# Where two-tile blocks keep the parts of their tokens in an SBUF buffer

## The chip, the cores and the metric

The kernel runs on one core of one Trainium2 chip. The metric is the device time of one execution in microseconds; for repeated executions the median is given. A profile is one execution with the hardware profiler on; its span runs from the first to the last instruction on the core.

## The reference

The computation is one block of a network on 2048 tokens of width 448, in float32:

- a conditioning vector gives six rows of 448 values (two shifts, two scales and two gates) by a matrix product;
- the tokens are normalised over their width, scaled and shifted, and convolved along the sequence with a kernel that comes from a state-space model; gated, this is added to the tokens;
- the sum is normalised, scaled and shifted again, and goes through a gated feed-forward layer: `(silu(h @ w_gate) * (h @ w_up)) @ w_down`, with 448 x 1792 gate and up weights and 1792 x 448 down weights; gated, this is added again.

The feed-forward layer is the large part, and it is the part that the change is in.

## The kernel before

The 2048 tokens are 16 tiles of 128. They go through the feed-forward layer in six blocks: the first two have two tiles (256 tokens), the last four have three (384 tokens). The hidden width of 1792 is 14 slices of 128, numbered f.

Precision comes from splitting. A value is kept as a high part, in TensorE's one-pass 32-bit format, and a low part, the rest. A product of two values is made of three products: high x high, high x low, low x high. The tokens of a block, transposed so that channels lie on partitions, stand in two SBUF tiles: `hhi` (high parts) and `hlo` (low parts), each of shape 128 x 4 x 384, where the second index k is the group of channels. A weight slice `gu` holds seven 128 x 128 matrices for the gate and seven for the up weights.

For each slice f the function `gate_up` computes the gate and the up product, s = 0 and 1. For each s there are seven matmuls with `hhi` and four with `hlo`, all recorded at line 754. The weights are loaded into the array as the stationary operand (128 columns), and the tokens stream past as the moving operand: 256 columns in a two-tile block, 384 in a three-tile block. So one slice takes 2 x 11 = 22 matmuls. After it, `down` (line 804) adds the slice f - 1 to the outputs: for each tile of the block three matmuls, with the hidden values (`phi`, `plo`) as the stationary operand and 448 columns of down weights (`wdh`, `wdl`) as the moving one. Between slices, single steps for the next block are put in after the slice's matmuls by a table of times: the convolution (lines 976 to 989) and, ahead of the last `down` of a block, the transposes of the next block's tokens (line 227 in one form). The order on TensorE is thus the order of the program. The other engines split weights (lines 115 to 125), apply the activation and split the hidden values (lines 769 to 792).

At the end of the last block `finish` (line 832) does the last two slices of the down product in pieces of 448, 256 and 192 columns, so that results leave earlier. They too have `phi` or `plo` as the stationary operand and down weights as the moving one.

Where a tile lies in SBUF is counted in bytes from the start of a partition. In this program `hhi` and `hlo` begin at bytes 48736 and 54880, both 96 modulo 256; every `gu` tile begins at 32 modulo 256, and so do all `wdh` and `wdl` tiles; `phi` and `plo` begin at 224 modulo 256. The matrices in `gu` (512 bytes each), the groups k in `hhi` (1536 bytes), and the tiles in `phi` (512 bytes) are all multiples of 256 bytes apart, so that a pair of tiles has one distance modulo 256. Counted from the moving to the stationary operand, it is

- (32 - 96) mod 256 = 192 for gate/up in a three-tile block;
- (32 - 224) mod 256 = 64 for gate/up in a two-tile block, since there the tokens begin at column 32 of the buffer, that is at byte 96 + 128 = 224;
- (224 - 32) mod 256 = 192 for the down products, in every block and in `finish`.

Where the parts are written: `high`, `high_v` and `low` for the first block's tokens, `split_turned` for the second block's, `transposes` for all others (lines 219 and 220 inside).

Of the kernel before, what the change touches and what calls it, by code (L numbers as in the profile page):

```python
# [51 lines left out]
def f32(ap):  # L52
    return ap.bitcast(F32)
# [3 lines left out]
def tile_kernel(ctx, tc, x, a_re, a_im, b_re, b_im, c_re, c_im, log_dt,  # L57
                wd, wgate_up, states, groups, vecs, dft, idft, out):
    nc = tc.nc
    sy, ve, sc, po, pe = nc.sync, nc.vector, nc.scalar, nc.gpsimd, nc.tensor  # L60
# [10 lines left out]
    def bank():  # L71
        t = psg.tile([128, 512], F32, name="bank")
        return t
# [38 lines left out]
    def split_d(j, part=None):  # L112
        hi, lo = wp[j]
        if not part:
            sc.copy(hi, wdn[j])
        if part != 0:
            ve.tensor_tensor(lo, wdn[j], f32(hi), op=OP.subtract)

    def split_w(j, part):
        w = raw[j]  # L120
        if part == 0:
            sc.copy(wgu[j][:, :, 0:3, :], w[:, :, 0:3, :])  # L122
            sc.activation(wgu[j][:, :, 3, :], w[:, :, 3, :], AF.Copy, scale=half)  # L123
        else:
            ve.tensor_tensor(wgu[j][:, :, 3:7, :], w[:, :, ::-1, :], f32(wgu[j][:, :, 0:4, :][:, :, ::-1, :]), op=OP.subtract)  # L125
# [18 lines left out]

    sbc = const.tile([128, 4], F32)
    flag = const.tile([1, 1], I32)
    first_col = lambda n: 32 if n == 256 else 0
    hhi = const.tile([128, 4, MB * 128], F32R)
    hlo = const.tile([128, 4, MB * 128], F32R)
    gd = const.tile([128, D], F32)  # L150
# [67 lines left out]
    def parts(hi, lo, src, k):  # L218
        sc.activation(hi, src, AF.Identity, bias=sbc[:, k:k + 1])
        ve.scalar_tensor_tensor(lo, src, sbc[:, k:k + 1], f32(hi), op0=OP.add, op1=OP.subtract)  # L220

    def transposes(ts):
        n = len(ts) * 128
        for k in (0, 2, 1, 3):
            ps = CV if k == 2 else bank()
            for j, i in enumerate(ts):
                pe.transpose(ps[:, j * 128:(j + 1) * 128], xn[i][:, k * 128:(k + 1) * 128], ident)  # L227
            c_ = slice(first_col(n), first_col(n) + n)
            parts(hhi[:, k, c_], hlo[:, k, c_], ps[:, 0:n], k)

    xd = [dram.tile([128, 512], F32, name=f"xd{q}") for q in range(MB)]
# [10 lines left out]
    def split_turned(ts):  # L242
        n, m = len(ts) * 128, len(ts)
        for k in range(4):
            hi, lo = (h[:, k, first_col(n):first_col(n) + n].rearrange("p (q a r) -> p q a r", q=m, a=4) for h in (hhi, hlo))
            parts(hi, lo, turned[:, 0:m, :, k, :], k)

    wp0 = ctx.enter_context(tc.tile_pool(name="wp0", bufs=1))
# [38 lines left out]
    with tc.tile_pool(name="pre", bufs=1) as pre:  # L287
# [153 lines left out]

        def high(q, ks=range(4)):
            for k in ks:
                c_ = slice(32 + q * 128, 160 + q * 128)
                sc.activation(hhi[:, k, c_], pk[q, k][:, k * 128:(k + 1) * 128], AF.Identity, bias=sbc[:, k:k + 1])

        def high_v(q, ks):
            for k in ks:
                c_ = slice(32 + q * 128, 160 + q * 128)
                ve.tensor_scalar(hhi[:, k, c_], pk[q, k][:, k * 128:(k + 1) * 128], sbc[:, k:k + 1], None, op0=OP.add)  # L450

        def low(q, ks=range(4)):
            for k in ks:
                c_ = slice(32 + q * 128, 160 + q * 128)
                ve.scalar_tensor_tensor(hlo[:, k, c_], pk[q, k][:, k * 128:(k + 1) * 128], sbc[:, k:k + 1], f32(hhi[:, k, c_]),
                                        op0=OP.add, op1=OP.subtract)

# [9 lines left out]
        def flag_of():  # L467
# [49 lines left out]
            "fr1": copy(run1[end], CV[end, 0:D]), "fx": copy(xs[0], DN[0][:, 0:D]),  # L517
            "tr0": do(to_channels, 0), "tr1": do(to_channels, 1, (0, 1)), "tr1b": do(to_channels, 1, (2, 3)),
            "hi00": do(high, 0, (0, 1)), "hi01": do(high_v, 0, (2, 3)),
            **{f"hi1{z}": do(high, 1, (2 * z, 2 * z + 1)) for z in range(2)},  # L520
            **{f"lo{q}{z}": do(low, q, (2 * z, 2 * z + 1)) for q in range(2) for z in range(2)},

            "w0": do(split_w, 0, 0), "w01": do(split_w, 0, 1), "w1": do(split_w, 1, 0), "w11": do(split_w, 1, 1),
# [206 lines left out]
    def run_blocks(pools, stages, first=None):  # L730
        work, hid = pools.work, pools.hid
        def ffn(ts, fresh, last, todo):
            n = len(ts) * 128
# [3 lines left out]
            def gate_up(f, nw):  # L737
                head = fresh and f < 2
                if fresh and f:
                    split_d(f)  # L740
                w = wgu[f]
                p = hid.tile([128, 280], F32, name="p") if fresh else p_of[f % 2]
                hi = hid.tile([128, MB * 128], F32R, name="phi")
                lo = hid.tile([128, MB * 128], F32R, name="plo")
                ps = [bank(), bank()]

                top = [(k, a) for k, ws in enumerate(((0, 6), (1, 5), (2, 4), (3,))) for a in ws]
                low = [(k, k) for k in range(4)]  # L750

                def mm(s, ka, lo, first=False, end=False):
                    for q, (k, a) in enumerate(ka):
                        pe.matmul(ps[s][:, 0:n], w[:, s, a], (hlo if lo else hhi)[:, k, first_col(n):first_col(n) + n],  # L754
                                  start=first and q == 0, stop=end and q == len(ka) - 1)

                if head:
                    for k in range(3):
                        for s in range(2):
                            mm(s, [(k, k)], False, k == 0)  # L760
                    for s in range(2):
                        mm(s, [(k, 6 - k) for k in range(3)] + [(3, 3)], False)
                    for s in range(2):
                        mm(s, low, True, False, True)
                else:
                    for s in range(2):
                        mm(s, top, False, True)
                        mm(s, low, True, False, True)
                sc.activation(p[:, 0:n], ps[0][:, 0:n], AF.Silu)  # L769
                for g, a in todo.get((f, 2), []):  # L770
                    g(*a)
                pp[f] = hi, lo
                if last and f == NF - 1:
                    c_ = [slice(q * 128, (q + 1) * 128) for q in range(len(ts))]
                    for q in range(len(ts) + 1):
                        for o in c_[q:q + 1]:
                            ve.tensor_tensor(ps[1][:, o], p[:, o], ps[1][:, o], op=OP.mult)
                            sc.copy(hi[:, o], ps[1][:, o])
                        for o in c_[max(q - 1, 0):q]:
                            ve.tensor_tensor(lo[:, o], ps[1][:, o], f32(hi[:, o]), op=OP.subtract)  # L780
                    return
                if nw is not None:
                    split_w(nw, 0)
                ve.tensor_tensor(ps[1][:, 0:n], p[:, 0:n], ps[1][:, 0:n], op=OP.mult)  # L784
                if fresh and f == 0:
                    split_d(0, 1)
                    for g, a in todo.get("mid", []):
                        g(*a)
                elif nw is not None:
                    split_w(nw, 1)  # L790
                sc.copy(hi[:, 0:n], ps[1][:, 0:n])  # L791
                ve.tensor_tensor(lo[:, 0:n], ps[1][:, 0:n], f32(hi[:, 0:n]), op=OP.subtract)  # L792
                if fresh and f == 0:
                    split_w(nw, 1)
# [11 lines left out]
            m = len(ts) - 1  # L806
# [64 lines left out]
        if first is not None:  # L871
            for i in TILES[1]:
                load_x(i)
            for i in TILES[0]:
                first(i)
                n2.stat(i, TILES[0])
            n2.root(TILES[0])
            for q, i in enumerate(TILES[0]):
                make_xn(i, work.tile([128, 512], F32, name=f"xn{q}"))
            transposes(TILES[0])  # L880
        for b, ts in enumerate(TILES):
            todo = {}
            if b + 1 < len(TILES):
# [40 lines left out]
                if late:  # L924
                    go(late[0], n2.root, nx)
                    for q, (h, i) in enumerate(zip(late[1], nx)):
                        if b:
                            go(h, make_xn, i, xn_of[q])
                        else:
                            go(h, make_xn, i, xn_of[q], 0)  # L930
                            at(NF - 2, 2, make_xn, i, xn_of[q], 1)
                at(NF - 1, 0, transposes if late else split_turned, nx)
            ffn(ts, b == 0, b + 1 == len(TILES), todo)

# [151 lines left out]
def build(nc, aps, out):  # L1086
    with tile.TileContext(nc) as tc:
        a = dict(aps)
        tile_kernel(tc, a["A_u"].rearrange("b l d -> (b l) d"), *[a[n] for n in _INS[1:] + ["B_w_gate_up", "A_states", "w_mod_groups", "c_log_dt", "dft", "idft"]],
                    out.rearrange("b l d -> (b l) d"))  # L1090
# [20 lines left out]
```

## Time and profile before

| | |
|---|---|
| median of 3 runs | 471.81 us (471.29 to 472.66) |
| profiled execution | 471.9 us, span 469.8 us |
| granted TensorE clock | 0.999 of full speed |
| matmuls at line 754 | 616 with 256 columns, 1232 with 384 columns |
| slices of two-tile blocks | 28 (two blocks of 14) |

The span is what the core's instructions cover, 2.1 us less than the time of that execution. Two kinds of answers matter below. The chain of waits gives the work that ended last, in order of time: start, length, engine and line, and how many instructions in a row were merged; on it the length of a merged row divided by its count is the distance from one instruction to the next. The timeline gives each group's start, its length up to the modelled end of its last instruction, the operation, the tiles and the shape. Matmuls are pipelined, so a matmul's own duration there is much longer than the distance to the next one: distances are taken from start to start.

### The profile page before, as it was taken

Reading aid. Unit: us, or ns where it says so; the run is one execution under the profiler, and the core shown is the slowest. Engines: PE = TensorE matmul, PEld = TensorE weight load, DVE = VectorE, ACT = ScalarE, POOL = GpSimd, SP = SyncE. Lnnn points to the kernel's source line nnn. Section 1 sums busy time; section 2 is a strip of 40 time slices with the busy share of each in tenths; the row PEclk is TensorE's granted clock in tenths of the full one; section 3 lists DMA queues with packets and bytes.
Section 4 is the critical chain, followed back from the end, with each engine's and each line's share of the span. In section 5 each row is a group of like instructions: output and inputs, shape, how many; then the busy total and the mean of one; then the engine's idle time right before and its main releaser. Section 6 shows DMA issues by size and latency. Waiting matters only on the chain.

```text
span 469.8 us, 7027 instructions
## 1 busy us (share of the span) xinstructions
PE 460.1 (98%) x2735; PEld 438.2 (93%) x2735; DVE 282.6 (60%) x540; ACT 160.1 (34%) x359; POOL 61.6 (13%) x88
## 2 busy tenths in 40 slices
PE   6999999999999999999999999999999999999995
PEld 3669999999999999999999999999999999999995
DVE  4888999778866447573754766464666543222124
ACT  5879666512343222233212223311223222221111
POOL 1122001000000223200022410004141000000000
PEclk9999999999999999999999999999999999999999
DMA  8976653110003000111300011130000112000001
GB/s 303 407 254 179 204 183 102 58 42 2 2 0 100 0 1 0 46 46 46 117 2 0 2 45 46 45 119 1 1 22 24 46 45 80 22 1 1 1 0 65
DMA packets 18779, 31.24 MB, mean 67 GB/s; under 512 B 2608, under 2 KB 13488, under 8 KB 18736
## 3 DMA queue, kind: packets, MB, share of 16 engines
q1 hardware_dynamic: 18096, 30.53, 19.2%
q8 instruction: 23, 0.38, 0.4%
q10 hardware_dynamic: 640, 0.18, 0.2%
q14 instruction: 20, 0.16, 0.1%
HBM read 24.61 MB, written 6.03 MB: 65 GB/s over the span
## 4 chain that ended last, share of the span: by engine, by line
PE 95%; DMA 3%; DVE 1%; SPq 0%; ACT 0%; issue 0%; DVEq 0%
PE bank L754 61%; PE dn L804 28%; DMA wm<-in_w_mod_groups_dram 2%; DMA vec<-in_c_log_dt_dram 1%; PE dn L476 1%; PE bank L256 1%; PE bank L977 1%; PE cv L976 1%; PE cv L978 1%; PE bank L227 0%; SPq L300 0%; DVE x L843 0%; PE bank L394 0%; PE cv L989 0%; PE bank L266 0%; PE bank L269 0%
## 5 line engine op out<-in xcount | busy, mean ns | idle before, releaser
L754 PE MATMUL bank<-hhi,gu 128*128 128x384 f32 (+1 forms) x1176 | 208.9, 317 | 0.2 <-issue 0.2
L754 PEld LDWEIGHTS bank<-hhi,gu 128*128 128x128 f32 x1176 | 189.4, 188 | 3.1 <-issue 1.1
L754 PE MATMUL bank<-hlo,gu 128*128 128x384 f32 (+1 forms) x672 | 130.8, 317 | 0.0
L754 PEld LDWEIGHTS bank<-hlo,gu 128*128 128x128 f32 x672 | 109.1, 188 | 0.2
L784 DVE TENSOR_TENSOR bank<-raw,bank 128x384 f32<-128x384 f32 (+1 forms) x69 | 36.8, 534 | 117.8 <-PE bank L754 115.5
L791 ACT CAST phi<-bank 128x384 fp32r<-128x384 f32 (+1 forms) x83 | 36.8, 444 | 138.9 <-DVE bank L784 138.8
L769 ACT ACTIVATE raw<-bank 128x384 f32<-128x384 f32 (+1 forms) x70 | 32.9, 470 | 119.3 <-PE bank L754 103.7
L792 DVE TENSOR_TENSOR plo<-bank,phi 128x384 fp32r<-128x384 f32 (+1 forms) x83 | 42.5, 511 | 37.6 <-ACT phi L791 37.6
L804 PE MATMUL dn<-wdh,phi 128*128 128x448 f32 x218 | 57.2, 364 | 0.0
L804 PE MATMUL dn<-wdh,plo 128*128 128x448 f32 x218 | 57.1, 362 | 0.0
L804 PE MATMUL dn<-wdl,phi 128*128 128x448 f32 x218 | 56.9, 362 | 0.0
L804 PEld LDWEIGHTS dn<-wdh,plo 128*128 128x128 f32 x218 | 40.9, 187 | 2.7
L804 PEld LDWEIGHTS dn<-wdl,phi 128*128 128x128 f32 x218 | 40.9, 187 | 2.7
L804 PEld LDWEIGHTS dn<-wdh,phi 128*128 128x128 f32 x218 | 38.6, 188 | 1.2
L185 POOL TENSOR_SCALAR rsb<-mvb 128x1 f32<-128x1 f32 (+2 forms) x13 | 4.6, 354 | 142.0 <-DVE mvb L157 142.0
L125 DVE TENSOR_TENSOR gu<-raw,gu 128x1024 fp32r<-128x1024 f32 x14 | 17.1, 1219 | 1.2 <-ACT gu L123 1.2
L185 POOL TENSOR_SCALAR rsa<-mva 128x3 f32<-128x3 f32 (+1 forms) x6 | 2.3, 381 | 98.7 <-DVE mva L157 96.4
L951 POOL TENSOR_TENSOR m<-m,gm 128x448 f32<-128x448 f32 x9 | 10.4, 1155 | 20.8 <-DVE m L202 17.1
L965 DVE TENSOR_TENSOR vl<-m,vh 128x448 fp32r<-128x448 f32 x12 | 9.1, 757 | 6.7 <-ACT vh L964 6.1
L122 ACT CAST gu<-raw 128x768 fp32r<-128x768 f32 x14 | 11.7, 833 | 0.0
L970 POOL TENSOR_TENSOR m<-m,gd 128x448 f32<-128x448 f32 x9 | 11.5, 1280 | 0.0
L215 ACT ACTIVATE raw<-raw,rsb 128x64 f32<-128x64 f32 x14 | 4.8, 345 | 18.9 <-DVE raw L212 9.7
(243 smaller groups left out, 410.2 us busy)
## 6 DMA issues: line engine op xcount, KB each, us to landing
raw<-in_B_w_gate_up_dram SPq DMA_DIRECT2D x14, 512.0 KB, 3.8
rawd<-in_B_w_down_dram SPq DMA_DIRECT2D x16, 224.0 KB, 3.9
x<-in_A_u_dram SPq DMA_DIRECT2D x12, 224.0 KB, 2.9
out_dram<-x SPq DMA_DIRECT2D x11, 224.0 KB, 2.0
xd<-raw SPq DMA_DIRECT2D x9, 256.0 KB, 2.0
raw<-xd SPq DMA_DIRECT2D x36, 64.0 KB, 1.9
wm<-in_w_mod_groups_dram SPq DMA_DIRECT2D x5, 448.0 KB, 8.2
wm<-in_w_mod_groups_dram SPq DMA_DIRECT2D x5, 336.0 KB, 8.2
```

The costliest lines, as they stand in the source:

```text
L122: sc.copy(wgu[j][:, :, 0:3, :], w[:, :, 0:3, :])
L125: ve.tensor_tensor(wgu[j][:, :, 3:7, :], w[:, :, ::-1, :], f32(wgu[j][:, :, 0:4, :][:, :, ::-1, :]), op=OP.subtract)
L185: po.tensor_scalar(rs[:, 0:n], self.mv[:, 0:n, 1], EPS, None, op0=OP.add)
L754: pe.matmul(ps[s][:, 0:n], w[:, s, a], (hlo if lo else hhi)[:, k, first_col(n):first_col(n) + n], start=first and q == 0, stop=end and q = ...
L769: sc.activation(p[:, 0:n], ps[0][:, 0:n], AF.Silu)
L784: ve.tensor_tensor(ps[1][:, 0:n], p[:, 0:n], ps[1][:, 0:n], op=OP.mult)
L791: sc.copy(hi[:, 0:n], ps[1][:, 0:n])
L792: ve.tensor_tensor(lo[:, 0:n], ps[1][:, 0:n], f32(hi[:, 0:n]), op=OP.subtract)
L804: pe.matmul(dn[q][:, 0:D], u[:, cs], v, start=f == 0 and z == 0, stop=f == (NF - 3 if last else NF - 1) and z == 2)
L951: (ve if on_v else po).tensor_tensor(v, h, g, op=OP.mult)
L965: ve.tensor_tensor(vl, v0, f32(vh), op=OP.subtract)
L970: (ve if on_v else po).tensor_tensor(h, h, gd, op=OP.mult)
```

## The change

Blocks of two tiles keep the parts of their tokens at column 0 of the buffers, not at column 32. All places that write or read these columns follow. Three-tile blocks are at column 0 in both kernels. No instruction is added or removed, no shape changes, and no tile moves: in two-tile blocks alone the moving operand of line 754, and what ScalarE and VectorE write for it, begins at byte 96 modulo 256 in place of 224.

```diff
-    first_col = lambda n: 32 if n == 256 else 0
...
-            c_ = slice(first_col(n), first_col(n) + n)
+            c_ = slice(0, n)
             parts(hhi[:, k, c_], hlo[:, k, c_], ps[:, 0:n], k)
...
-            hi, lo = (h[:, k, first_col(n):first_col(n) + n].rearrange("p (q a r) -> p q a r", q=m, a=4) for h in (hhi, hlo))
+            hi, lo = (h[:, k, 0:n].rearrange("p (q a r) -> p q a r", q=m, a=4) for h in (hhi, hlo))
             parts(hi, lo, turned[:, 0:m, :, k, :], k)
...
-                c_ = slice(32 + q * 128, 160 + q * 128)
+                c_ = slice(q * 128, (q + 1) * 128)
                 sc.activation(hhi[:, k, c_], pk[q, k][:, k * 128:(k + 1) * 128], AF.Identity, bias=sbc[:, k:k + 1])
...
-                        pe.matmul(ps[s][:, 0:n], w[:, s, a], (hlo if lo else hhi)[:, k, first_col(n):first_col(n) + n],
+                        pe.matmul(ps[s][:, 0:n], w[:, s, a], (hlo if lo else hhi)[:, k, 0:n],
                                   start=first and q == 0, stop=end and q == len(ka) - 1)
```

The line in the third hunk is changed alike in `high`, `high_v` and `low`.

More of the change, by code (lines that the diff above doesn't have):

```diff
@@ L448, in high_v @@
             for k in ks:
-                c_ = slice(32 + q * 128, 160 + q * 128)
+                c_ = slice(q * 128, (q + 1) * 128)
                 ve.tensor_scalar(hhi[:, k, c_], pk[q, k][:, k * 128:(k + 1) * 128], sbc[:, k:k + 1], None, op0=OP.add)
@@ L453, in low @@
             for k in ks:
-                c_ = slice(32 + q * 128, 160 + q * 128)
+                c_ = slice(q * 128, (q + 1) * 128)
                 ve.scalar_tensor_tensor(hlo[:, k, c_], pk[q, k][:, k * 128:(k + 1) * 128], sbc[:, k:k + 1], f32(hhi[:, k, c_]),
```

## The prediction

> **What bounds the kernel now.** I read the page first: busy time, the granted clock, and the chain of work that ended last.
>
> ```profile
> span 469.8 us, 7027 instructions
> PE 460.1 (98%) x2735; PEld 438.2 (93%) x2735; DVE 282.6 (60%) x540; ACT 160.1 (34%) x359; POOL 61.6 (13%) x88
> PEclk9999999999999999999999999999999999999999
> PE 95%; DMA 3%; DVE 1%; SPq 0%; ACT 0%; issue 0%; DVEq 0%
> ```
>
> TensorE (PE) carries 95% of the chain at full clock, and its weight loads (PEld) are almost as busy as its matmuls. So the distance from one matmul to the next is the time of this kernel. The waits, filtered for TensorE, say that line 754 hardly ever waits for another engine:
>
> ```profile
> PE bank L754 <- issue: 0.2, 1, 0.2
> ```
>
> The groups by line and shape give the number of matmuls that the change touches, those with 256 columns:
>
> ```profile
> L754 PE MATMUL bank<-hhi,gu 128*128 128x256 f32 x392 | 54.7, 280 | 0.2 <-issue 0.2
> L754 PE MATMUL bank<-hlo,gu 128*128 128x256 f32 x224 | 34.9, 279 | 0.0
> ```
>
> 392 + 224 = 616 = 28 slices x 22. Their mean duration (280 ns) is no price, since matmuls overlap: distances are needed. The chain in order of time, taken for the two-tile blocks alone, gives them, because there it consists of TensorE alone: a row's length over its count is the mean distance. First and last rows of its kinds:
>
> ```profile
> 32.86 5.76 PE bank L754 x44
> ...
> 39.82 2.51 PE bank L754 x22
> ...
> 58.35 2.51 PE bank L754 x22
> 60.86 1.20 PE dn L804 x6
> ...
> 62.27 0.75 PE cv L989 x2
> 63.02 2.60 PE bank L754 x22
> 65.61 1.21 PE dn L804 x6
> 66.83 2.59 PE bank L754 x22
> ...
> 71.68 2.60 PE bank L754 x22
> ...
> 75.49 2.59 PE bank L754 x22
> ...
> 79.29 2.52 PE bank L754 x22
> ...
> 88.81 5.18 PE bank L754 x44
> ...
> 95.20 2.52 PE bank L754 x22
> ...
> 137.87 2.51 PE bank L754 x22
> ```
>
> The reader is to see that the same 22 matmuls on the same shapes take two different times. Twenty rows (39.82 the first, 137.87 the last) last 2.51 or 2.52 us, mean 2.513: 114.2 ns per matmul, which I call narrow. Six slices (63.02, 66.83, 71.68, 75.49 and the two in the row of 44 at 88.81) take 15.56 us together, 2.593 each: 117.9 ns, wide. TensorE waits in neither. The wide ones start after something else has run on TensorE than the usual product (line 989 before 63.02, the start of a block at 88.81), and stay wide for slices until they drop back. So a pair of streams, the tokens and the next weights, has at least two stable paces at one distance of 64 bytes. That makes it plausible that a distance of 192 has others.
>
> **The change, part by part.** *The writes.* Lines 219, 220 and those of the first block's tokens write the same shapes 128 bytes earlier; the count is equal. Ahead of the second block they run beside its predecessor's last down products:
>
> ```profile
> 87.26 0.48 ACT L219 ACTIVATE hhi<-cv,sbc 128x256 fp32r<-128x256 f32 x1
> 88.20 0.87 DVE L220 SCALAR_TENSOR_TENSOR hlo<-bank,sbc,hhi 128x256 fp32r<-128x256 f32 x2
> 88.64 0.99 PE L754 MATMUL bank<-hhi,gu 128*128 128x256 f32 x7
> 89.47 0.40 PE L754 MATMUL bank<-hlo,gu 128*128 128x256 f32 x2
> ```
>
> The last low part ends at 88.20 + 0.87 = 89.07 and is read from 89.47 on: 0.40 us of cover, which is what a slower write would have to eat first. I set the writes to nothing. Without cover, a tenth on each of a block's eight writes of some 0.48 us would be 0.4 us, once in each of two blocks.
>
> *Waits and queues.* No instruction moves on any engine, no transfer is issued at another place, and so nothing is queued behind anything new. Three-tile blocks are untouched.
>
> *The matmuls.* The whole price is the distance between 256-column matmuls at 192 bytes in place of 64. The kernel shows 192 bytes in two places already. The first is line 754 in three-tile blocks, with the very tiles of the change, but 384 columns; line 804 has 448 columns at the same distance (timeline, start and length of each group):
>
> ```profile
> 199.76 1.38 PE L754 MATMUL bank<-hhi,gu 128*128 128x384 f32 x7
> 200.97 0.86 PE L754 MATMUL bank<-hlo,gu 128*128 128x384 f32 x4
> 201.66 1.38 PE L754 MATMUL bank<-hhi,gu 128*128 128x384 f32 x7
> 202.88 0.86 PE L754 MATMUL bank<-hlo,gu 128*128 128x384 f32 x4
> 203.57 0.36 PE L976 MATMUL cv<-vh,tri 128*128 128x448 f32 x1
> ...
> 204.18 0.76 PE L804 MATMUL dn<-wdh,phi 128*128 128x448 f32 x3
> ...
> 205.98 0.69 PE L754 MATMUL bank<-hhi,gu 128*128 128x384 f32 x3
> ```
>
> From 199.76 to 203.57 are 22 matmuls: 173.2 ns each. From 204.18 to 205.98 are nine: 200.0 ns each. The difference, 26.8 ns for 64 columns, is 0.419 ns a column, so 256 columns alone are 107 ns, and both rows carry about 13 ns on top of their columns. The narrow pace carries 7, the wide 11. A straight line through both rows gives 119.6 ns at 256 columns.
>
> The second place is the tail, line 832, which has 256 columns at 192 bytes, with other tiles:
>
> ```profile
> 462.87 0.28 PE L832 MATMUL cv<-wdh,phi 128*128 128x256 f32 x1
> ...
> 463.22 0.36 PE L832 MATMUL bank<-wdh,phi 128*128 128x448 f32 x1
> ...
> 463.83 0.28 PE L832 MATMUL cv<-wdh,phi 128*128 128x256 f32 x1
> ...
> 464.18 0.25 PE L832 MATMUL dn<-wdh,phi 128*128 128x192 f32 x1
> ...
> 464.72 0.27 PE L832 MATMUL dn<-wdh,plo 128*128 128x192 f32 x1
> ```
>
> Three matmuls take 0.35 us twice: 0.70 / 6 = 117 ns, with 2 ns of rounding either way. That has the shape and the distance of the changed kernel, and it is the wide pace, not the narrow one. I take the wide pace, 117.9, for all 616. It isn't sure: three in a row are few, and at 64 bytes too there are wide stretches, which end.
>
> Below, the five 192-column distances from 464.18 to 464.72 bound it: 0.54 / 5 = 108 ns, though fewer columns stream. There the weight load sets the pace, and no matmul with a new 128-column load can be expected much under that. So the price lies between 108 and 119.6 ns.
>
> *Sum.* The twenty narrow slices and the second slice of the first row of 44 (I count it as narrow) go from 2.513 to 2.593 us: 21 x 0.080 = 1.7 us. The six wide ones stay. The slice of heads at 32.86 waits for its inputs and I leave it. The chain is TensorE's alone from there to the end, so that all of it arrives: 471.9 + 1.7 = 473.6 us for the profiled execution. Its 471.9 (469.8 of span and 2.1 around it) is 0.1 over the median of 471.81, so 473.5 us against the median, or +0.36%. What hides work in these blocks gets more time, not less.
>
> **A rule of the Trainium skill against it.** The rows are those above: one pair of tiles, one shape, 2.51 and 2.60 us without a wait. The Trainium skill, page "SBUF — State Buffer", section "Who interferes with whom", gives TensorE two independent read ports, one for the moving operand and one for the weight load, and says that it never waits on anyone. By that rule the place of an operand modulo 256 does nothing and the sum is 471.8 us. The two paces don't contradict the rule outright, but neither does it explain them; it is the third rival's mechanism below.
>
> **The rivals.**
>
> *Both rows' 13 ns come along (slower still).* Weights load only during the first part of a 384-column matmul, since a load can be done in 108 ns of its 173 (above). If what the two streams lose falls in that part, the first 256 columns lose all 13 ns and the distance is 119.6 ns, 2.63 us a slice. For it speaks that the tiles and the distance are exactly those of the change; against it, that the tail's 448-column rows have 13 ns at 192 bytes and its 256-column rows 10. Price: 21 x 0.118 + 6 x 0.038 = 2.7 us, 474.5 us.
>
> *The pair takes the narrow pace all through, or the mixture stays (no difference).* The tail's six would then be a start-up. Narrow everywhere is 6 x 0.080 = 0.5 us less, 471.3; the mixture stays at 471.8. For it: two paces exist at one distance, so distance alone doesn't choose. Against it: the tail's six distances are wide in their mean, while after `down` most slices at 64 bytes are narrow.
>
> *The loss goes away (faster).* The mechanism: at 192 bytes the two streams stay clear of each other for the whole of 256 columns, and the weight load alone sets 108 ns. The place is the same 616 matmuls. A slice is then 2.38 us, and the sum 21 x 0.137 + 6 x 0.217 = 4.2 us, 467.6 us. It decides from 0.1 us per slice on. What would hold it back is VectorE in the first block:
>
> ```profile
> 32.80:85.40 52.60, 52.54 (x387) 50.48 (x388) 49.52 (x90) 37.87 (x88) 5.39 (x10) 1.00 0.51 159
> 86.10:140.40 54.30, 54.30 (x406) 53.11 (x405) 42.24 (x87) 17.31 (x43) 2.23 (x4) 1.00 0.07 22
> ```
>
> After the stretch and its length stand the busy times of PE, PEld, DVE, ACT and POOL. DVE is busy for 49.52 of 52.60 us in the first block, so a faster TensorE would soon wait for split weights there; only the second block's 12 narrow and 2 wide slices are sure: 12 x 0.137 + 2 x 0.217 = 2.1 us, 469.7 us. For it speaks only that 108 is not reached now; against it every 192-byte row of the trace.
>
> The Trainium skill, page "TensorE: Matmul & The Clock Gate", section "Back-to-back issue gap", gives columns over 2.4 plus 2.5 ns for a warm stream, an estimate of 109 ns at 256 columns; no row here of 256, 384 or 448 columns reaches that form.
>
> **How the numbers follow.** About 0.3%, 1.4 us, is what a measurement of this kernel can tell from no change. Wide everywhere (473.5): 0.42. It is so near the bound that I give 0.11 of this to a reading within 0.3%. The full 13 ns (474.5): 0.24, a little of it, 0.04, for still more than that. Narrow or mixed (471.3 to 471.8): 0.20. Faster (467.6 to 469.7): 0.14. So slower 0.31 + 0.24 = 0.55, within 0.3% 0.20 + 0.11 = 0.31, faster 0.14. The range leaves out the faster rival and what lies past the 13 ns, 0.18 together: from 471.3 less 0.4 for the runs' spread, 470.9, to 474.5 plus 0.6, 475.1 us.
>
> **What would show it.** In the changed kernel's chain the rows of 22 at line 754 between 39 and 142 us last 2.59 to 2.60 us, all of them; 2.63 means the first rival, 2.51 the second, 2.38 the third. The three-tile rows stay at 3.81 us for 22, the down rows at 1.20 for six. DVE and ACT keep their means. It would be wrong if the rows alternate between paces as now, if a third pace appears that no row of this trace has, or if the granted clock differs.

## The result, and the profile after

The changed kernel takes 472.94 us (median of 13 runs), the kernel before 471.52 us (13 runs): a ratio of 1.0032, 95% interval 1.0024 to 1.0040. It is slower, by about the 1.5 us that 0.32% are. Two of its 13 executions took 474.7 and 474.9 us; why they were longer is not known. The prediction was 473.5 us, +0.36%.

The page of the changed kernel, the busy times and the chain by engine: the span and TensorE's busy times have grown, and the other engines are within 1 us of before.

```profile
span 470.9 us, 7027 instructions
PE 462.4 (98%) x2735; PEld 440.7 (94%) x2735; DVE 282.9 (60%) x540; ACT 160.1 (34%) x359; POOL 62.5 (13%) x88
PEclk9999999999999999999999999999999999999999
PE 95%; DMA 3%; DVE 1%; SPq 0%; ACT 0%; issue 0%; DVEq 0%
```

The chain in order of time over the two-tile blocks (start, length, engine and line, count; line 753 here is line 754 of the kernel before), first and last rows of their kinds:

```profile
32.73 5.85 PE bank L753 x44
...
39.78 2.59 PE bank L753 x22
...
63.55 2.59 PE bank L753 x22
...
89.37 5.18 PE bank L753 x44
...
95.76 2.59 PE bank L753 x22
...
139.34 2.59 PE bank L753 x22
141.93 0.33 PE bank L226 x3
```

All 24 rows of 22 between these last 2.59 us, and the row of 44 twice that: these are the 26 two-tile slices after the first two, which share the row at 32.73. There is no narrow slice left; the kernel before had twenty. The three-tile blocks are the same: their slices are 3.81 us in every single row before, and 3.81 or, in seven rows, 3.82 after. Their first rows, of the kernel before and of the changed one:

```profile
144.32 7.63 PE bank L754 x44
...
153.75 3.81 PE bank L754 x22
```

```profile
145.66 7.63 PE bank L753 x44
...
155.09 3.81 PE bank L753 x22
```

So where did the time come from? The two-tile blocks last from 32.86 to 140.38 us before, 107.52 us, and from 32.73 to 141.93 after, 109.20 us: +1.68 us. The rows of line 754 make 1.60 of it (71.59 us in all before, 73.19 after). The span grew by 1.1 only. The rest of the sum is in places that the change doesn't touch: the first product began 0.13 us earlier, the transposes and down products ahead of block three took 0.21 us less (from 140.38 to 144.32, and from 141.93 to 145.66), and what follows the last sums was 0.24 us shorter. From the start of block three to the last sums both kernels take 319.33 us. Here are the transposes and the start of the last sums, before and then after:

```profile
140.38 0.33 PE bank L227 x3
...
141.04 0.87 PE bank L227 x6
...
463.65 1.73 DVE x L843 x4
```

```profile
142.59 0.66 PE bank L226 x6
...
464.99 1.72 DVE x L842 x4
```

From 463.65 to the span's end of 469.8 are 6.15 us, from 464.99 to 470.9 are 5.91. Such tenths vary from execution to execution: in the runs below the first product of line 754 starts anywhere between 32.5 and 34.0 us. For that reason the experiments are read by the length of slices, which repeats to some 0.02 us at one distance and pace, and not by single times of whole executions.

### The profile page after: what moved, and what is told of

It is laid out like the page before. It is cut to its first block, busy times and chain, and to the rows that moved or that the text cites. A ratio compares the mean times of both kernels' runs of the same rounds, so it can differ in the third digit from the quotient of the medians.

```text
span 470.9 us, 7027 instructions
## 1 busy us (share of the span) xinstructions
PE 462.4 (98%) x2735; PEld 440.7 (94%) x2735; DVE 282.9 (60%) x540; ACT 160.1 (34%) x359; POOL 62.5 (13%) x88
## 4 chain that ended last, share of the span: by engine, by line
PE 95%; DMA 3%; DVE 1%; SPq 0%; ACT 0%; issue 0%; DVEq 0%
PE bank L753 61%; PE dn L803 28%; DMA wm<-in_w_mod_groups_dram 2%; DMA vec<-in_c_log_dt_dram 1%; PE dn L475 1%; PE bank L255 1%; PE bank L976 1%; PE cv L977 1%; PE cv L975 1%; DVE x L842 0%; PE bank L226 0%; PE cv L988 0%; PE bank L393 0%; PE bank L265 0%; SPq L299 0%; PE bank L268 0%
```

## The experiments

The theory: the distance modulo 256 bytes from the moving tokens to the stationary weights allows certain paces; 64 allows the narrow one (2.51 us for 22 gate/up matmuls), 192 doesn't. Rivals: the absolute place of the tokens; the column itself; a longer period than 256; or that only the history of the stream counts. Each experiment is one profiled execution.

**Is the period 256 bytes?** Two more columns, at the same distances modulo 256 but not modulo 512:

```diff
-    first_col = lambda n: 32 if n == 256 else 0
+    first_col = lambda n: 64 if n == 256 else 0
...
-                c_ = slice(32 + q * 128, 160 + q * 128)
+                c_ = slice(64 + q * 128, 192 + q * 128)
```

> The kernel before with the tokens of two-tile blocks at column 64, not 32: 192 bytes modulo 256, as at column 0, but 448 modulo 512 where column 0 has 192. Theory (the distance between the tokens and the weights modulo 256 sets the pace): every slice of 22 matmuls in a two-tile block takes 2.59 us, as at column 0, and the span is near 470.9 us. Rival (a longer period than 256 bytes, or the column itself counts): another pace, such as the mixture of 2.51 and 2.59 us of the kernel before or one that neither kernel has.

> The kernel before with the tokens of two-tile blocks at column 96: 64 bytes modulo 256, as at column 32, but 320 modulo 512 where column 32 has 64. Theory (distance modulo 256): most slices of 22 at 2.51 us, some stretches at 2.59, as in the kernel before, span near 469.8 us. Rival (a longer period, or the column itself): all 2.59 us or a third pace.

The second has 96 in place of 64 in both lines. In the chain of the kernel with column 64 every slice after the first two is 2.59 us (one row 2.60):

```profile
34.03 5.86 PE bank L754 x44
...
41.10 2.59 PE bank L754 x22
...
136.86 2.59 PE bank L754 x22
```

With column 96 the mixture is back: 22 narrow slices (one of them 2.53), and four wide ones (two single, two in the row of 44).

```profile
58.82 2.51 PE bank L754 x22
...
63.48 2.59 PE bank L754 x22
67.29 2.59 PE bank L754 x22
72.04 2.51 PE bank L754 x22
...
89.14 5.18 PE bank L754 x44
95.53 2.52 PE bank L754 x22
```

Both as the theory had it; a period of 512 would have made them two new distances. The spans are 472.4 and 470.2 us. That of column 64 is over the expected 470.9 because its first product began at 34.03 us, 1.3 us later than in the changed kernel. That delay was there before the edit could act: the matmuls of line 266 start at 28.35 us (27.18 in the kernel before, whose first product starts at 32.86), and the first part of a token is written at the new column at 33.05.

**Is it the distance, or where the tokens stand?** Three kernels. The first keeps column 0 and moves the weights:

```diff
+    gap = const.tile([128, 32], F32)
     gd = const.tile([128, D], F32)
...
-                p = hid.tile([128, 280], F32, name="p") if fresh else p_of[f % 2]
+                p = hid.tile([128, 264], F32, name="p") if fresh else p_of[f % 2]
```

> Tokens at column 0 as in the changed kernel, and 128 unused bytes behind the tokens' buffers, so that all weights lie 128 bytes later (160 modulo 256). So that the buffers still fit, the scratch tile p of the hidden pool is 264 columns wide, not 280; the hidden values stay where they were. Gate/up is then at 64 bytes in every block, three-tile ones too, and the down products are at 64 bytes, not 192. Theory (distance): two-tile slices return to mostly 2.51 us though the tokens stand where the changed kernel has them. Rival (the absolute place of the tokens, byte 96 modulo 256, counts): all slices stay at 2.59 us. Beside that, the 13 ns that 384 and 448 columns carry: if they belong to 192 bytes, three-tile slices fall from 3.81 us (22 x 173.2 ns) to about 3.67 (22 x 167) and the whole kernel gets some 8 us faster; if any distance costs two losses there, 3.81 us stays and the span is near 469.8 us.

```profile
40.05 2.51 PE bank L755 x22
42.55 1.21 PE dn L805 x6
43.76 2.59 PE bank L755 x22
46.36 1.21 PE dn L805 x6
47.57 2.51 PE bank L755 x22
...
89.20 5.19 PE bank L755 x44
...
138.83 2.59 PE bank L755 x22
```

The narrow pace is back, with the tokens where the changed kernel has them: 11 narrow slices of 26, against none. So the rival that byte 96 forbids it falls. But the theory's "mostly" was a miss: over long stretches narrow and wide slices alternate one by one. The down products, which run between the slices, stand at 64 here and not at 192. The next kernel has tokens and weights at the same bytes modulo 256 as this one, the down products at 192, and no such alternation, so it goes with where the hidden values stand; how that acts isn't shown. The other half of the expectation missed too: of the single rows of three-tile slices 32 are 3.82 us and 15 are 3.88, and nothing is near 3.67.

The second moves everything and leaves all distances as they were before:

```diff
-    tok = const.tile([128, 1], F32)
+    halves = const.tile([128, 6], F32)
+    mhalf, half, ones, pick, tok, ntok = (halves[:, q:q + 1] for q in range(6))
...
-    ones = const.tile([128, 1], F32)
-    halves = const.tile([128, 2], F32)
-    mhalf, half = halves[:, 0:1], halves[:, 1:2]
-    ntok = const.tile([128, 1], F32)
-    pick = const.tile([128, 1], F32)
```

> The kernel before, with six one-column constants of 128 x 1 put into one tile, which frees 128 bytes, so that tokens, weights and hidden values all lie 128 bytes earlier. The tokens of two-tile blocks, at column 32, then stand at byte 96 modulo 256, where the changed kernel has them; every distance between two tiles (64 for gate/up in two-tile blocks, 192 for the down products) is as in the kernel before. Theory (only distances count): the mixture of the kernel before again, some twenty slices of 2.51 us and a few of 2.59, span near 469.8 us. Rival (the absolute place counts): 2.59 us throughout, span near 470.9 us.

```profile
39.73 2.51 PE bank L750 x22
...
62.93 2.59 PE bank L750 x22
...
88.72 5.18 PE bank L750 x44
```

Twenty-one slices are narrow, five are wide (three single rows of 2.59 and a row of 44 at 5.18), and the span is 469.4 us. With equal distances the kernel before is there again, though each tile stands at another place. The third is the changed kernel with the same packing of constants and the `gap` of 128 bytes behind the buffers, so that of the operands of the gate, up and down products only the tokens move:

> The changed kernel (column 0), with the same 128 bytes freed ahead of the tokens' buffers and 128 unused bytes behind them: the buffers begin at 224 modulo 256, all else stays. Two-tile gate/up is at 64 bytes with the tokens at column 0; three-tile gate/up is at 64 too, the down products stay at 192. Theory (distance): two-tile slices are those of the kernel before, mostly 2.51 us. Rival (the column, or what the shorter step of the writes does): 2.59 us. Three-tile slices: 3.81 us, since the moved weights showed 13 ns or more at 64 bytes too; slices of 3.88 us, which appeared there, would come back if they belong to the distance of gate/up, and stay away if they were due to the down products at 64.

Of its 26 two-tile slices 22 are narrow, at column 0. Its chain, the last two-tile slice and some of the three-tile blocks:

```profile
137.88 2.51 PE bank L751 x22
...
144.35 7.77 PE bank L751 x44
153.92 3.88 PE bank L751 x22
...
177.26 3.82 PE bank L751 x22
```

So neither the column nor the shorter step of the writes makes the 2.59 us. And the 3.88 us of three-tile slices (38 of 47 single rows are 3.88 or 3.89, nine are 3.82) belong to their own distance of 64, since the down products are at 192 here. That costs more than the change itself: the execution takes 475.24 us beside 471.73 of the kernel before on the same chip. The packing alone (the second kernel, 471.56 us beside the same 471.73) shows no cost.

**Which distances are good for 256 columns?** Columns 16, 24, 40 and 48, edited as column 64 above:

> The kernel before with the tokens of two-tile blocks at column 16: 128 bytes modulo 256. The theory says that the distance decides but not which pace 128 has: 2.51 us throughout would be some 0.5 us under the kernel before, 2.59 us throughout the changed kernel, 2.63 us the 13 ns of the longer matmuls. The rival that distance does nothing, and that the history of the stream alone sets the pace, expects the mixture of 2.51 and 2.59 us again.

> The kernel before with the tokens of two-tile blocks at column 24: 96 bytes modulo 256, between 64 (mixture of 2.51 and 2.59 us) and 128 (2.60 to 2.63 us). If the pace goes smoothly with the distance, a slice lies between these, 2.54 to 2.60 us; if the loss is one of whole steps, slices take one of the paces seen, 2.51, 2.59 or 2.60, and nothing between. The rival that distance does nothing expects the mixture of the kernel before.

> The kernel before with the tokens of two-tile blocks at column 40: 32 bytes modulo 256. If 64 bytes is the middle of a favourable stretch, 32 is as 96; if the narrow pace is favoured by any small distance, slices are 2.51 us throughout and the kernel is 0.5 us faster than before. The rival that distance does nothing expects the mixture.

> The kernel before with the tokens of two-tile blocks at column 48: 0 bytes modulo 256. After 32, 96, 128 and 192 bytes all gave mean distances of 117.8 to 118.6 ns, the theory that 64 is one favoured place and all others lose expects 2.58 to 2.63 us a slice. The rival that an aligned pair is a second favoured place expects 2.51 us or less.

The chains of the four, in this order (128, 96, 32 and 0 bytes):

```profile
40.07 2.61 PE bank L754 x22
43.89 2.60 PE bank L754 x22
...
132.39 2.63 PE bank L754 x22
```

```profile
40.05 2.61 PE bank L754 x22
43.86 2.58 PE bank L754 x22
```

```profile
40.21 2.61 PE bank L754 x22
44.03 2.61 PE bank L754 x22
```

```profile
39.55 2.63 PE bank L754 x22
...
140.05 2.64 PE bank L754 x22
```

No slice of 2.51 us is in any of them, and so the history of the stream alone doesn't set the pace. At 128 bytes slices take 2.60 to 2.63, at 96 they mostly alternate between 2.58 and 2.61 (one 2.62), at 32 they take 2.60 or 2.61, at 0 they take 2.63 or 2.64. So the whole-step expectation for 96 (only 2.51, 2.59 or 2.60) was wrong, and so was the thought that 64 is the middle of a broad good stretch: 32 bytes to either side of it the narrow pace is gone. The rival of a second favoured place at 0 falls as well. The executions at these four took 1.8 to 3.1 us more than the kernel before on the same chip. The kernel before stands at the best of the six distances tried.

**Can the three-tile blocks win by another distance?** Constants packed as above, a gap of 16, 8 or 24 columns behind the buffers, and two-tile blocks at column 48, 40 or 56, which keeps these at 64 bytes:

```diff
+    gap = const.tile([128, 16], F32)
     gd = const.tile([128, D], F32)
...
+    first_col = lambda n: 48 if n == 256 else 0
```

> Constants packed as in the run with all tiles moved, 64 unused bytes behind the tokens' buffers, two-tile blocks at column 48: gate/up at 64 bytes in two-tile blocks as before, and at 0 in three-tile blocks; down products at 192 as before. Two-tile slices: mostly 2.51 us (distance theory). Three-tile slices: 3.81 us if the 13 ns of the longer matmuls don't depend on the distance except for a bad place at 64 (3.88 us); under 3.75 us if another distance can halve them as 64 does with 256 columns, which would be some 4 to 8 us of the whole; over 3.85 us if 192 is the one good place of 384 columns, as 64 is that of 256.

> The same with 32 unused bytes and column 40: gate/up at 64 in two-tile blocks, at 224 in three-tile blocks. Expectations as in the run at 0: 3.81 us a slice if the distance does nothing there but at 64, under 3.75 if it can halve the loss, over 3.85 if 192 is the one good place.

> The same with 96 unused bytes and column 56: gate/up at 64 in two-tile blocks, at 32 in three-tile blocks. Expectations as in the run at 0: 3.81 us a slice, under 3.75, or over 3.85.

The first single slices of their three-tile blocks, at 0, 224 and 32 bytes:

```profile
153.82 3.84 PE bank L751 x22
```

```profile
153.34 3.88 PE bank L751 x22
```

```profile
153.63 3.82 PE bank L751 x22
```

None is under 3.81. At 0, 41 single rows are 3.84 and six 3.82; at 224, 44 are 3.88 and three 3.89; at 32, 41 are 3.82 and six 3.83. The two-tile slices, at 64 in all three, were mostly narrow again. The hope for 4 to 8 us is refuted for these distances, and 192 is again the best tried, though 32 is within 0.01 us a slice. The times, 472.79, 475.32 and 472.02 us, stand beside 472.83 of the kernel before on the same chip. Single executions as near as the first and the last can't be told from it. The one at 224 is 2.5 us longer, as its slices are: 0.07 us on each of 56 would be 3.9. In that execution VectorE, too, came onto the chain in the first block, but block two began no later for it (88.48 us, against 88.81 before). No version clearly beats the kernel before.

The slices by distance, all from rows of these chains, in two-tile blocks without the first two:

| bytes, modulo 256 | 22 matmuls of 256 columns, us | 22 of 384 columns, us |
|---|---|---|
| 0 | 2.63, 2.64 | 3.84 (six of 3.82) |
| 32 | 2.60, 2.61 | 3.82 (six of 3.83) |
| 64 | 2.51, in stretches 2.59 | 3.82 and 3.88 |
| 96 | 2.58 and 2.61, mostly in turn | not tried |
| 128 | 2.60 to 2.63 | not tried |
| 192 | 2.59 | 3.81 (some of 3.82) |
| 224 | not tried | 3.88 |

## Why the prediction was right

- **What bounds the kernel.** Right. The chain is TensorE's before and after, the clock is the same, and 0.08 us on a slice is 0.08 us on the chain. The signs that it named came as named: 2.59 us in every slice, three-tile rows at 3.81, down rows at 1.20 or 1.21, no new pace.
- **The writes, waits and queues at nothing.** Right: VectorE and ScalarE have the busy times of before (282.6 and 160.1 us then, 282.9 and 160.1 now), and the column alone changed nothing once the buffer moved along with it.
- **The price.** Right: 2.59 us a slice, 117.7 ns, at this distance at column 0 and again at column 64. Forecast from slices 1.7 us, measured 1.60 in the rows of line 754. The slice that I counted as narrow inside the first row of 44 went as counted: 5.76 to 5.85 us.
- **Where the price came from.** Here there was luck. The wide pace was taken from six matmuls of the tail. Two stretches of 0.35 us, each between two starts rounded to 0.01, leave 3 ns of doubt on 117, not 2; the narrow pace, 114.2, and the full loss, 119.6, both lie within that. And the tail doesn't keep one pace at 192 bytes. The changed kernel has its tail at the same distance and with the same shapes, and there the first three matmuls of 256 columns take 0.36 us and the second three 0.34, which is 113 ns and thus narrow:

```profile
464.20 0.28 PE L831 MATMUL cv<-wdh,phi 128*128 128x256 f32 x1
...
464.56 0.37 PE L831 MATMUL bank<-wdh,phi 128*128 128x448 f32 x1
...
465.17 0.28 PE L831 MATMUL cv<-wdh,phi 128*128 128x256 f32 x1
...
465.51 0.25 PE L831 MATMUL dn<-wdh,phi 128*128 128x192 f32 x1
```

The second three are narrow in the tails of column 40 and of the runs with three-tile blocks at 224 and 32 bytes as well, and wide in most of the others. So 192 bytes exclude the narrow pace for gate/up, where the chain shows none in 26 slices, but not for every pair of tiles. By the prediction's own sum this tail gives 0.70 / 6 = 117 ns again, though half of it is narrow: the mean couldn't tell the paces apart.

- **The 13 ns.** At 0.419 ns a column the rows of 384 and 448 columns carry 12.4 ns, not 13. The tail's three of 448 columns, from 463.22 to 463.83 us, carry some 16, with 3 of doubt. The forecast doesn't rest on either.
- **That all of it arrives at the end.** Right in kind; in this pair of executions 0.58 us were made up outside the two-tile blocks by differences that the other runs show without the change too. The medians, 1.42 us apart, lie between the 1.1 us of the spans and the 1.68 of the two-tile blocks. The measured 0.32% is barely over the 0.3% that the prediction took as the least that can be told from no change.
- **The rivals.** The full loss on 256 columns (2.63 us) does exist, at 0 bytes and in two slices at 128, but not at 192; the straight line through 384 and 448 columns was no guide to 192. The narrow pace throughout, or a mixture, needs the distance of 64 in gate/up: at 192 not one slice had it. The fast rival's 108 ns, 2.38 us a slice, appeared in none of thirteen changed kernels. Its neighbour, the estimate of 109 ns, uses the form that the Trainium skill, page "TensorE: Matmul & The Clock Gate", section "Back-to-back issue gap", gives for an isolated matmul. In the streams here, each matmul with new weights, the narrow slices of 256 columns have 114 ns in the mean.
- **The rule of the page "SBUF — State Buffer"** (the Trainium skill, section "Who interferes with whom"), by which TensorE has two independent read ports and never waits on anyone: as the prediction read it, the place would have cost nothing. The same matmuls took from 2.51 to 2.64 us here with no wait in the chain, as the distance was changed. The measurement decides. The 471.8 us of this rule are the price of the second rival, not of the third, to which the prediction refers.

What stays open. Whether the reads of the tokens and of the weights get in each other's way, and which of them then loses, no row shows: only the pace of both together is seen. What makes a slice at 64 bytes wide is seen only by its company (after line 989, at a block's start, and in turn with narrow ones where the down products stood at 64); no mechanism is shown. Other work alone isn't enough: before 122.41 us lines 976 to 978 run in the kernel before, and that slice is narrow, 2.52 us. In every kernel where most slices are narrow, the tokens of two-tile blocks stand at the same byte modulo 256 as the hidden values (224 in the kernel before), since 64 and 192 add up to 256. Only the kernel with the moved weights has 64 bytes without that, and there wide and narrow took turns. What this place does by itself was not tried. Distances that aren't multiples of 32 bytes, 160 and 224 for 256 columns, and 96, 128 and 160 for 384 were not tried.

## What to carry to other kernels

Where TensorE alone is the chain, look at the distance from matmul to matmul in steady rows, not at their durations: two lengths of the same group of matmuls without a wait were here the sign of something that an address changes. The place of the moving and of the stationary tile to each other modulo 256 bytes was worth up to 5% of 256-column matmuls here (2.51 to 2.64 us), and the best place differed between 256 and 384 columns, so it has to be tried per shape. A change ahead of a buffer (a packed constant, a wider scratch tile) can shift it without anybody having meant to.

## What was unexpected

A pace holds over whole slices. At one distance of 64 bytes the same 22 matmuls last 2.51 or 2.59 us, and which of the two seems to depend on how the slice begins: with the down products at 64 bytes, narrow and wide slices took turns (2.51, 2.59, 2.51 in the rows of the moved weights).

The good places are sharp and not shared. At 64 bytes 256 columns are fastest (2.51), and 384 columns take 3.88 us in most slices with the moved buffers and in a third with the moved weights; at 192 it is 2.59 and 3.81. Moving the buffer to give both shapes the 64 bytes cost 3.5 us (475.24 against 471.73 us, one execution of each), more than twice the change studied.
